# Adaptive-norm attention and gated FFN on one core: couple terms placed between the pairs of score tiles, with transfers in small parts

## The chip, the cores and the metric

The kernel runs on one core of one Trainium2 chip. The metric is device time in microseconds of one execution, the median of several runs. The kernel is written in Bass with Tile: the program names instructions and tiles, Tile adds the waits, and the order on TensorE (PE), VectorE (DVE), ScalarE (ACT) and of the transfers that SyncE (SP) issues is pinned to the program's order by small wrappers (`pe`, `dve`, `act`, `sp1`). [...]

## The reference, cut to what matters

The input is one sequence of 2048 rows of 512. Attention has 32 query heads of width 16 over a single key and value head; the FFN has a width of 1792.

```python
mod = (silu(c) @ w_mod).reshape(c.shape[0], 6, 1, -1)
sa, ca, ga, sb, cb, gb = mod[:, 0], ..., mod[:, 5]
h = layernorm(x) * (1 + ca) + sa
x = x + ga * A(h, A_wq, A_wk, A_wv, A_wo)        # q per head, one k, one v; softmax(q k / 4) v; @ wo
h = layernorm(x) * (1 + cb) + sb
x = x + gb * B(h, B_w_gate, B_w_up, B_w_down)    # (sigmoid(h Wg) * (h Wu)) Wd
```

Products of float32 operands are formed of float16 high and low parts in three passes (high x high, high x low, low x high), except the product of the probabilities with V, which is in float32.

## The kernel before, in words

**Stages.** A prologue (the word list `PLAN`) computes the modulation rows, the first norm, K, V and part of Q. A main loop then runs over 32 units: a unit is a block of 256 query rows (8 blocks) with one of 4 groups of 8 heads. A unit has 16 steps, one per 128 keys, and a step has two halves, here called pieces: 1024 pieces in all. An epilogue computes the last block's output projection and FFN with the whole 128x128 array.

**Attention in a piece.** The array is used as two halves of 64 rows, each with four column tiles of 32, so that a product 64x128x512 is a set of four matmuls side by side (`columns`, L137 to 139). `ORDER` (`"a0", "s0", "c", "a1", "s1"`) sets a piece: two score tiles `a` for the row maxima of a later unit (written to banks `sa`, three of them, reduced by DVE, `a_max`), two score tiles `s` with the keys on partitions (banks `st`, two of them, exponentiated by ACT into `P`, `st_tile`), and between the pairs `c`, the product of V with the probabilities of the step pair before (`pv`), into the one bank `craw`. The score tiles of a piece all stand on one array half; `pv` stands on the other, `side[0]`. Which is which changes at every second step (`sides`). [...]

**Couple terms.** Projections and the FFN of the blocks that are through with attention fill in. A `Couple` is two `Group`s (two row tiles) that run together, one on each array half; after half of its terms the two groups change halves (`g = self.gs[j ^ (n >= m)]`), behind a hand-over. A term is one set on either half. Per block there are: the output projection `wo` (24 terms, banks `po`), 7 gate-up couples `gu` (24 terms each, banks `pgu`) and two down couples `dn` (banks `pd`) of the hidden chunks below and from `HF` up: 48 and 36 terms with `HF = 8`. In `ffn_block`, the line `gs.insert(NCH, gs.pop(NCH - 1))` puts the first down couple ahead of the seventh gate-up couple. `pace` and `places` spread the terms over pieces at a rate of at least `LEAST` 2 and at most `MOST` 3, so that a block's work ends `CHAIN` 26 steps into the next block. `pick` takes a couple once all its inputs in `needs` are marked and `GAP` 2 steps have passed. `piece` plans and then issues one part of the running couple, after the piece's score tiles:

```python
for n in range(n0, n1):
    ...
    for j in (1 - side[0], side[0]):
```

**What comes between.** When a couple ends, its two banks are evicted by ACT and DVE (for `gu`: `th` twice and `u` once on ACT, `u` once on DVE). POOL then makes the float16 rows `gr`, which a transposing transfer on SP turns (`turned`, 3 steps later, `GLATE`). After `wo`, POOL and DVE do the second norm (`norm`, `norm2`, `norm3`, each deferred by steps) and make rows `h2r`, which are turned the same way (`HLATE`); a mark is set when the transfer is issued. Gate-up weights come from DRAM (`wD`) as 1 MB chunks into two buffers (`ask`, one transfer per chunk, issued as the couple before opens).

**Weights.** `weight_jobs` splits the FFN weights into high and low parts on POOL (L333 to L335) and stores gate and up to `wD`; 42 of the 46 jobs are spread over the first `WSTEPS` = 90 steps of the main loop.

Of the kernel before, what the change touches and what calls it, by code (L numbers as in the profile page):

```python
# [61 lines left out]

SKIP = 9
GAP = 2
CHAIN = 26
QRATE = 1.1
MOST = 3
# [1 line left out]
HELD = 60  # L69
SWAP = 5  # L70
FRESH = 0.9
WSTEPS = 90
WLAST = 100
WLATE = 2
WSTORE = 5
# [17 lines left out]
def adaln_mqa_glu_kernel(  # L93
# [100 lines left out]
    class Couple:  # L194
        def __init__(self, a, c):
            self.gs, self.stage, self.w, self.n = (a, c), a.stage, a.w, 2 * a.n

        def part(self, n0, n1):
            if n0 == 0:
                for g in self.gs:  # L200
                    g.open()
            m = self.gs[0].n
            for n in range(n0, n1):
                if n == m:
                    assert self.since is not None or done[0] > self.marks
                    take_over(self.since)
                for j in (1 - side[0], side[0]):
                    g = self.gs[j ^ (n >= m)]
                    l_, r_, *cut = g.term(n % m, slice(64 * j, 64 * j + 64))
                    columns(cut[0](g.bank) if cut else g.bank, l_, r_, n == 0, n == 2 * m - 1)  # L210
                if n == m - 1:
                    self.since, self.marks = None, done[0]
                    if open_[0]:
                        hand_over()
                        self.since = done[0]
            if n1 == self.n:
                for k, g in enumerate(self.gs):
                    g.end(g.bank, k == 1)
# [576 lines left out]

    use, gws = [0], {}

    def ask(upto):
        while use[0] <= upto:
            k = use[0]  # L800
            gws[k] = gw_tile()
            sp1.dma_start(gws[k], wD[CH[k % NCH]])
            use[0] += 1

    def ffn_block(b, end_of_all=False):
        x1, xrs, h2, ups, ths, gT = {}, {}, {}, {}, {}, {}
        at = b * NCH
        HF = 8

        def wo_group(t):  # L810
            def term(n, rs):
                o, i = divmod(n, 3)
                a_, w_ = passes(*aTs[b, o], WO['woh'], WO['wol'])[i]
                return a_[rs, t * P:(t + 1) * P], w_[rs, o, :]

            def begin():
                xrs[t] = t32("xr")
                sp1.dma_start(xrs[t], x[b * QU + t * P:b * QU + (t + 1) * P, :])

            def end(po, second):  # L820
                xr, t1 = xrs.pop(t), t32("t1")
                if second:
                    act.activation(t1, po, AF.Identity)
                    pool.tensor_tensor(t1, t1, mods[2], op=ALU.mult)
                else:
                    dve.tensor_tensor(t1, po, mods[2], op=ALU.mult)
                if tail:
                    dve.tensor_tensor(xr, t1, xr, op=ALU.add)
                    row_norm([t1], [xr])
                    dve.tensor_tensor(t1, t1, mods[4], op=ALU.mult)  # L830
                    dve.tensor_tensor(t1, t1, mods[3], op=ALU.add)
                    x1[t] = xr, t1
                else:
                    defer(1 + 2 * t, lambda: norm(t, t1, xr))

            return Group("wo", 12, "po", term, end, begin)

# [3 lines left out]

        def norm2(t, t1, xr):
            row_norm([t1], [xr], later=True)
            defer(1, lambda: norm3(t, t1, xr))

        def norm3(t, t1, xr):
            x1[t] = xr, t1
            pool.tensor_tensor(t1, t1, mods[4], op=ALU.mult)
            pool.tensor_tensor(t1, t1, mods[3], op=ALU.add)
            rows = pair("h2r")  # L850
            pool.tensor_scalar(rows[:, 0], t1, 1.0, 0.0, op0=ALU.mult, op1=ALU.add)
            pool.tensor_tensor(rows[:, 1], t1, rows[:, 0], op=ALU.subtract)
            h2[t] = turned(rows, f"h2{t}")
            if b == 0 and t == 0:
                ask(0)
            defer(HLATE, h2[t][1])

        def turned(rows, name):
            t_ = pair(name).rearrange("p a (c r) -> p (a c) r", r=P)

            def go():
                sp1.dma_start_transpose(t_, rows.rearrange("p a n -> p (a n)"))
                marks[b, name] = now[0]

            return t_, go

        def gu_group(c_, t):
            def begin():
                if t == 0:
                    ask(at + c_ + 1)  # L870
                    ths[c_], ups[c_] = t32("th"), t32("u")

            def term(n, rs):
                k, i = divmod(n, 3)
                gw = gws[at + c_]
                h_, w_ = ((0, 0), (1, 0), (0, 1))[i]
                return h2[t][0][rs, 4 * h_ + k, :], gw[rs, k, 2 * w_:2 * w_ + 2, :].rearrange("p m n -> p (m n)")

            def end(p_, second):
                ts = slice(256 * t, 256 * (t + 1))  # L880
                th, u_ = ths[c_], ups[c_]
                if second:
                    dve.tensor_copy(u_[:, ts], p_[:, 256:])
                    act.activation(th[:, ts], p_[:, :256], AF.Tanh, scale=0.5 / (SH * SW))
                else:
                    act.activation(th[:, ts], p_[:, :256], AF.Tanh, scale=0.5 / (SH * SW))
                    act.activation(u_[:, ts], p_[:, 256:], AF.Identity)
                if t == 1:
                    gated_rows(c_)

            return Group("gu", 12, "pgu", term, end, begin)

        def gated_rows(c_):
            th, u_ = ths.pop(c_), ups.pop(c_)
            pool.tensor_scalar(th, th, 1.0, 1.0, op0=ALU.add, op1=ALU.mult)  # L895
            pool.tensor_tensor(th, th, u_, op=ALU.mult)  # L896
            rows = pair("gr")
            pool.tensor_scalar(rows[:, 0], th, 1.0, 0.0, op0=ALU.mult, op1=ALU.add)
            pool.tensor_tensor(rows[:, 1], th, rows[:, 0], op=ALU.subtract)  # L899
            gT[c_], go = turned(rows, f"g{c_}")  # L900
            if tail:
                go()
            else:
                defer(GLATE, go)

        def gu_cols(c_, m):
            def begin():
                if m == 0:
                    ask(at + c_ + 1 if c_ < NCH - 1 else at + c_)

            def term(n, rs):
                e, (k, i) = n // 12, divmod(n % 12, 3)
                gw = gws[at + c_]
                h_, w_ = ((0, 0), (1, 0), (0, 1))[i]
                return gw[rs, k, 2 * w_ + m, e * P:(e + 1) * P], h2[k][rs, h_, :QU], lambda z: z[:, e * QU:(e + 1) * QU]

            def end(p_, second):
                if m == 0:
                    ths[c_] = th = t32("th")
                    act.activation(th, p_, AF.Tanh, scale=0.5 / (SH * SW))  # L920
                    return
                th, g_ = ths.pop(c_), pair("gc")
                dve.scalar_tensor_tensor(th, th, 1.0, p_, op0=ALU.add, op1=ALU.mult)
                pool.tensor_scalar(g_[:, 0], th, 1.0, 0.0, op0=ALU.mult, op1=ALU.add)
                pool.tensor_tensor(g_[:, 1], th, g_[:, 0], op=ALU.subtract)
                gT[c_] = g_

            return Group("gu", 24, "pgu", term, end, begin)
# [52 lines left out]
        for ds in downs:  # L981
            gs.append(Couple(*ds))
            gs[-1].needs = [(b, f"g{c_}") for c_ in (range(HF // 2) if len(gs) == NCH + 1 else range(NCH))]
        gs.insert(NCH, gs.pop(NCH - 1))
        first = Couple(*wos)
        for g in [first, *gs]:
            g.b = b
# [85 lines left out]
    def pick(s):  # L1073
        if urgent and s >= urgent[0].ready:
            return urgent.pop(0)
        if work and all(k in marks and s >= marks[k] + GAP for k in getattr(work[0], "needs", ())):
            return work.pop(0)

    def pace(s, g):
# [35 lines left out]
            at += z  # L1115
        assert at == g.n, (at, g.n, g.stage)

    def piece(s, h):
        plan(s, 2 * s + h)
        if run:  # L1120
            g, n0, n1 = run.pop(0)
            if n1 > n0:
                g.part(n0, n1)


    vq = []
# [2 lines left out]
    for i, (b, o) in enumerate(units):  # L1129
# [5 lines left out]
        for kb in range(NKB):  # L1135
# [13 lines left out]
            for n in range(2):  # L1149
                t = kb - kb % 2 + n  # L1150
                for z in ORDER:
                    k = int(z[1:] or 0)
                    if z[0] == "a" and an + 4 * n + 2 * k + 1 - h < len(alist):
                        a_tile(*alist[an + 4 * n + 2 * k + 1 - h])
                    if z == "c" and vq:
                        pv(*vq[n], second)
                    if z[0] == "s":
                        st_tile(i, t, k, 1 - h, second)
                if n == 0:
                    lows[:] = [z() for z in ready_rows]  # L1160
                piece(s, n)
                if n == 1:
                    for z in lows:
                        z()
# [8 lines left out]
                wdone += 1  # L1173
    assert wdone == nw and len(qdone) == 4 * NB
    while run:
        piece(s, 1)
    for n in range(4):
        pv(*vq[n % 2], n > 1)
    while waits:
        now[0] += 1  # L1180
        for z in [z for z in waits if z[0] <= now[0]]:
            waits.remove(z)
            z[1]()
    psum["ctx"].close()
    psum["ctx"] = ctx.enter_context(ExitStack())
    psum["b"] = psum["ctx"].enter_context(tc.tile_pool(name="pz", bufs=1, space=PSUM, reuse_waits="tile"))
# [47 lines left out]
```

## Time and profile before

| | |
|---|---|
| median of 3 runs | 1681.4 us (1678.07 to 1688.73) |
| the profiled execution | 1682.25 us |
| its span, first to last instruction | 1680.5 us |
| mean granted TensorE clock | 0.988 |
| PE, PEld busy | 1608.2 us, 991.0 us |
| DVE, ACT, POOL busy | 1419.8 us, 1305.5 us, 666.2 us |

In rows of the order of time, the first number is the start in us from the span's start, the second the time in us, then engine, line, operation, output and inputs, shape and count; a bracket gives the idle time before and what ended it. In the table by stretches a row gives the stretch, its length, then for PE, PEld (weight loads), DVE, ACT and POOL the busy time and the number of instructions, then the granted clock, the share of the DMA engines and GB/s. In the table of waits a row gives the total, the number of times and the longest. Nearly all instructions of PE, DVE, ACT and SP show line 139, that of a helper, so the tile names tell them apart.

### The profile page before, as it was taken

To read this page: it belongs to the slowest core of one execution; us is meant where nothing else is said; L and a number is where in the kernel's file an instruction comes from. 1 tells how busy PE (TensorE), PEld (TensorE's weight loads), DVE (VectorE), ACT (ScalarE), POOL (GpSimd) and SP (SyncE) were. 2 spreads that over 40 slices of the span, in tenths; PEclk is the share of its full clock that TensorE was granted. 3 is DMA by queue.
4 is the path that set the end of the run, shared out by engine and by line. 5 is a ranking of instruction groups with operands and counts; after the bars stand their busy time and mean duration, and the time that the engine had idled before them with its cause. 6 is when DMAs were issued, how large, how long until landed. Compare 5 with 4: busy or idle time off the path is not lost.

```text
span 1680.5 us, 91637 instructions
## 1 busy us (share of the span) xinstructions
PE 1608.2 (96%) x41477; PEld 991.0 (59%) x41477; DVE 1419.8 (84%) x2400; ACT 1305.5 (78%) x2409; POOL 666.2 (40%) x827
## 2 busy tenths in 40 slices
PE   6999999979999999999999999999999999999998
PEld 3335554436666566666566666666666666665465
DVE  7789999879999899999899999999899989993041
ACT  5549998768888888888888888888888888888600
POOL 4433756664315322362316331453226232442222
PEclk9989999989999999999999999999999999999999
DMA  7121433334321432233321341223322341233322
GB/s 243 57 69 43 126 130 125 93 99 127 85 59 28 113 81 52 57 89 84 78 59 35 116 104 24 59 86 83 82 59 65 84 103 54 29 112 83 108 76 75
DMA packets 145090, 140.18 MB, mean 83 GB/s; under 512 B 91332, under 2 KB 125116, under 8 KB 136636
## 3 DMA queue, kind: packets, MB, share of 16 engines
q1 hardware_dynamic: 144700, 134.32, 29.2%
q8 instruction: 325, 5.32, 1.3%
q14 instruction: 65, 0.53, 0.1%
HBM read 97.18 MB, written 16.24 MB: 67 GB/s over the span
## 4 chain that ended last, share of the span: by engine, by line
PE 81%; POOL 5%; ACT 4%; DVE 4%; DMA 3%; issue 2%; SPq 2%; POOLq 0%; ACTq 0%
PE craw L139 22%; PE pgu L139 17%; PE sa L139 16%; PE st L139 9%; PE pd L139 7%; PE po L139 3%; PE pgu L190 2%; PE pd L190 2%; PE pq L139 2%; DVE mx L139 2%; ACT P L139 2%; SPq L139 1%; POOL t L363 1%; DMA h<-h2r 1%; DMA xall<-in_A_x_dram 1%
## 5 line engine op out<-in xcount | busy, mean ns | idle before, releaser
L139 DVE TENSOR_REDUCE mx<-sa 128x1 f32<-128x512 f32 x2048 | 1310.0, 684 | 111.8 <-PE sa L139 56.3
L139 ACT ACTIVATE P<-st 128x512 f32<-128x512 f32 x2048 | 1180.5, 598 | 230.8 <-PE st L139 174.4
L139 PE MATMUL craw<-P,V 64*32 64x512 f32 x8192 | 1090.6, 598 | 2.1 <-issue 1.2
L139 PE MATMUL st<-qp,kp 64*32 64x512 f16 x8192 | 837.1, 380 | 11.3 <-ACT P L139 7.2
L139 PE MATMUL sa<-kp,qp 64*32 64x512 f16 (+1 forms) x7940 | 830.9, 379 | 8.9 <-DVE mx L139 5.5
L139 PEld LDWEIGHTS <-kp 64*32 64x32 f16 x8192 | 325.9, 91 | 262.5 <-issue 101.3
L139 PE MATMUL pgu<-gw,h 64*32 64x512 f16 x9408 | 422.2, 378 | 21.9 <-DMA h<-h2r 11.4
L139 PEld LDWEIGHTS <-qp 64*32 64x32 f16 (+1 forms) x7940 | 273.3, 92 | 139.7 <-issue 57.0
L139 PEld LDWEIGHTS <-h 64*32 64x32 f16 (+1 forms) x9600 | 211.8, 92 | 107.0 <-issue 41.7
L139 PEld LDWEIGHTS craw<-P,V 64*32 64x32 f32 x8192 | 194.8, 105 | 24.2 <-issue 5.1
L895 POOL TENSOR_SCALAR th<-th 128x512 f32<-128x512 f32 x49 | 30.3, 618 | 368.7 <-ACT th L139 242.6
L139 PE MATMUL pd<-wdh,g 64*32 64x512 f16 x2688 | 132.8, 377 | 0.8
L563 POOL MEMSET qp<- 32x1024 f16 x60 | 56.7, 944 | 131.7 <-PE st L139 129.7
L139 PEld LDWEIGHTS <-g 64*32 64x32 f16 x4032 | 86.7, 92 | 33.9 <-issue 6.7
L139 PE MATMUL pd<-wdl,g 64*32 64x512 f16 x1344 | 80.1, 376 | 0.0
L896 POOL TENSOR_TENSOR th<-th,u 128x512 f32<-128x512 f32 x49 | 62.9, 1284 | 4.1
L333 POOL TENSOR_SCALAR wst<-wst 128x512 f32<-128x512 f32 x46 | 28.4, 618 | 86.3 <-DMA wst<-in_B_w_gate_dram 28.8
L139 DVE COPY u<-pgu 128x256 f32<-128x256 f32 x49 | 20.3, 415 | 49.8 <-PE pgu L139 22.5
L948 POOL TENSOR_TENSOR ot<-ot,gb 128x512 f32<-128x512 f32 x12 | 15.4, 1282 | 115.9 <-ACT ot L139 115.9
L899 POOL TENSOR_TENSOR gr<-th,gr 128x512 f16<-128x512 f32 x49 | 57.1, 1164 | 4.0
L139 PE MATMUL craw<-nought 64*32 64x1 f16 x353 | 57.8, 164 | 0.0
L139 PE MATMUL pq<-h,wdh 64*32 64x512 f16 (+1 forms) x688 | 53.8, 386 | 0.1
(156 smaller groups left out, 1139.0 us busy)
## 6 DMA issues: line engine op xcount, KB each, us to landing
gw<-wD SPq DMA_DIRECT2D x56, 1024.0 KB
wD<-gw SPq DMA_DIRECT2D x7, 1024.0 KB
wm<-in_w_mod_dram SPq DMA_DIRECT2D x6, 1024.0 KB
qp<-qD SPq DMA_DIRECT2D x192, 32.0 KB
qD<-q SPq DMA_DIRECT2D x16, 256.0 KB
xr<-in_A_x_dram SPq DMA_DIRECT2D x16, 256.0 KB
out_dram<-ot SPq DMA_DIRECT2D x16, 256.0 KB
raw<-cs SPq DMA_DIRECT2D x248, 16.0 KB
```

The lines of the kernel that those rows point to most:

```text
L139: return (lambda *a, **k: keep(f_(*a, **k))) if pinned else f_
L190: pe.matmul(cut[0](self.bank) if cut else self.bank, l_, r_, start=(n == 0), stop=(n == self.n - 1))
L333: pool.tensor_scalar(w_, w_, SW, 0.0, op0=ALU.mult, op1=ALU.add)
L363: eng.tensor_scalar(dst, src, mv[:, i, 0:1], rs[:, i:i + 1], op0=ALU.subtract, op1=ALU.mult)
L563: eng.memset(qp[j:j + 32], 0.0)
L895: pool.tensor_scalar(th, th, 1.0, 1.0, op0=ALU.add, op1=ALU.mult)
L896: pool.tensor_tensor(th, th, u_, op=ALU.mult)
L899: pool.tensor_tensor(rows[:, 1], th, rows[:, 0], op=ALU.subtract)
L948: pool.tensor_tensor(ot, ot, mods[5], op=ALU.mult)
```

## The change

1. `Couple.part` is split. A new `front` is called right after `pv`, between the two pairs of score tiles. If the part holds two terms or more and is not the first of its couple, `front` issues the sets of the first half of its terms (rounded up) on the score tiles' half, `1 - side[0]`. `part`, after the second pair, issues the other sets: those left on the score half, and all on the other half. The wait of the change of halves, `take_over`, moves into `front` where there is one.
2. Transposes are issued in four parts of two 128-column blocks, and the gate-up chunk is loaded in eight parts of 128 KB. One of these parts is issued at the end of each piece (`drip`), transposes first; `fetched` issues what is left of a chunk when its couple opens.
3. `HF` is 6 instead of 8 (the down couples have 36 and 48 terms), and the seventh gate-up couple is no longer moved behind the first down couple.
4. The second norm of the second row tile starts one step earlier (`1 + t` instead of `1 + 2 * t`), and `norm3` becomes part of `norm2`, one step earlier for both.
5. `WSTEPS` is 66 instead of 90. For the first block, gate-up couples wait `EGAP` = 6 steps behind the mark of `h21` instead of `GAP` = 2.

```diff
+EGAP = 6
-WSTEPS = 90
+WSTEPS = 66
...
+        def half(self, n, j):
+            m = self.gs[0].n
+            g = self.gs[j ^ (n >= m)]
+            l_, r_, *cut = g.term(n % m, slice(64 * j, 64 * j + 64))
+            columns(cut[0](g.bank) if cut else g.bank, l_, r_, n == 0, n == 2 * m - 1)
+
+        def front(self, n0, n1):
+            self.ahead = 0
+            if n0 == 0 or n1 - n0 < 2:
+                return
+            m = self.gs[0].n
+            assert n1 <= m or n0 >= m
+            if n0 == m:
+                assert self.since is not None or done[0] > self.marks
+                take_over(self.since)
+            self.ahead = (n1 - n0 + 1) // 2
+            for n in range(n0, n0 + self.ahead):
+                self.half(n, 1 - side[0])
+
         def part(self, n0, n1):
...
-            m = self.gs[0].n
+            m, k = self.gs[0].n, self.ahead
+            if n0 == m and not k:
+                assert self.since is not None or done[0] > self.marks
+                take_over(self.since)
             for n in range(n0, n1):
-                if n == m:
-                    assert self.since is not None or done[0] > self.marks
-                    take_over(self.since)
-                for j in (1 - side[0], side[0]):
-                    g = self.gs[j ^ (n >= m)]
-                    l_, r_, *cut = g.term(n % m, slice(64 * j, 64 * j + 64))
-                    columns(cut[0](g.bank) if cut else g.bank, l_, r_, n == 0, n == 2 * m - 1)
+                if n + k < n1:
+                    self.half(n + k, 1 - side[0])
+                self.half(n, side[0])
...
+    turns, loads = [], []
+
+    def drip():
+        if turns:
+            turns.pop(0)()
+        elif loads:
+            loads.pop(0)[1]()
+
+    def fetched(upto):
+        while loads and loads[0][0] <= upto:
+            loads.pop(0)[1]()
...
-            gws[k] = gw_tile()
-            sp1.dma_start(gws[k], wD[CH[k % NCH]])
+            gws[k] = gw = gw_tile()
+            for z in range(NDC):
+                for y in range(2):
+                    at = slice(2 * y, 2 * y + 2)
+                    loads.append((k, lambda gw=gw, k=k, z=z, at=at: sp1.dma_start(gw[:, z, at], wD[CH[k % NCH], :, z, at])))
...
-        HF = 8
+        HF = 6
...
-                    defer(1 + 2 * t, lambda: norm(t, t1, xr))
+                    defer(1 + t, lambda: norm(t, t1, xr))
...
-            defer(1, lambda: norm3(t, t1, xr))
-
-        def norm3(t, t1, xr):
             x1[t] = xr, t1
...
+            def part(z):
+                sp1.dma_start_transpose(t_[:, 2 * z:2 * z + 2], of[:, 2 * z * P:2 * (z + 1) * P])
+                if z == 3:
+                    marks[b, name] = now[0]
+
             def go():
-                sp1.dma_start_transpose(t_, rows.rearrange("p a n -> p (a n)"))
-                marks[b, name] = now[0]
+                turns.extend(lambda z=z: part(z) for z in range(4))
...
                 if t == 0:
+                    fetched(at + c_)
                     ask(at + c_ + 1)
...
-        gs.insert(NCH, gs.pop(NCH - 1))
...
-        if work and all(k in marks and s >= marks[k] + GAP for k in getattr(work[0], "needs", ())):
+        if work and all(k in marks and s >= marks[k] + (EGAP if k == (0, "h21") else GAP) for k in getattr(work[0], "needs", ())):
...
-    def piece(s, h):
+    def front(s, h):
         plan(s, 2 * s + h)
+        if run and run[0][2] > run[0][1]:
+            run[0][0].front(*run[0][1:])
+
+    def piece():
         if run:
             g, n0, n1 = run.pop(0)
             if n1 > n0:
                 g.part(n0, n1)
+        drip()
...
-                    if z == "c" and vq:
-                        pv(*vq[n], second)
+                    if z == "c":
+                        if vq:
+                            pv(*vq[n], second)
+                        front(s, n)
```

In the epilogue a transpose is issued whole as its four parts at once, and `gu_cols` issues the next chunk's eight parts as a chunk opens.

More of the change, by code (lines that the diff above doesn't have):

```diff
@@ L859, in turned @@
             t_ = pair(name).rearrange("p a (c r) -> p (a c) r", r=P)
+            of = rows.rearrange("p a n -> p (a n)")
+            def part(z):
+                sp1.dma_start_transpose(t_[:, 2 * z:2 * z + 2], of[:, 2 * z * P:2 * (z + 1) * P])
+                if z == 3:
+                    marks[b, name] = now[0]
             def go():
-                sp1.dma_start_transpose(t_, rows.rearrange("p a n -> p (a n)"))
-                marks[b, name] = now[0]
+                turns.extend(lambda z=z: part(z) for z in range(4))
             return t_, go
@@ L900, in gated_rows @@
             gT[c_], go = turned(rows, f"g{c_}")
-            if tail:
-                go()
-            else:
+            if not tail:
                 defer(GLATE, go)
+                return
+            go()
+            while turns:
+                drip()
         def gu_cols(c_, m):
@@ L909, in begin @@
                     ask(at + c_ + 1 if c_ < NCH - 1 else at + c_)
+                    fetched(at + c_ + 1)
             def term(n, rs):
@@ L1123, in piece @@
                 g.part(n0, n1)
+        drip()
     vq = []
@@ L1160, in adaln_mqa_glu_kernel @@
                     lows[:] = [z() for z in ready_rows]
-                piece(s, n)
+                piece()
                 if n == 1:
@@ L1175, in adaln_mqa_glu_kernel @@
     while run:
-        piece(s, 1)
+        front(s, 1)
+        piece()
     for n in range(4):
@@ L1183, in adaln_mqa_glu_kernel @@
             z[1]()
+    while turns or loads:
+        drip()
     psum["ctx"].close()
```

## The prediction

> **What bounds the kernel now.** First the page, then a table by stretches, then the order of the instructions in single stretches, then the table of waits.
>
> ```profile
> span 1680.5 us, 91637 instructions
> ```
>
> What the array can do is seen in the order of time of PE in one quiet stretch (start, busy us):
>
> ```profile
> 667.37 0.40 PE L139 MATMUL sa<-kp,qp 64*32 64x512 f16 x4
> 667.41 0.64 PE L139 MATMUL craw<-P,V 64*32 64x512 f32 x4
> 667.58 0.40 PE L139 MATMUL st<-qp,kp 64*32 64x512 f16 x4
> 667.80 0.40 PE L139 MATMUL sa<-kp,qp 64*32 64x512 f16 x4
> 667.86 0.61 PE L139 MATMUL craw<-P,V 64*32 64x512 f32 x4
> 668.01 0.40 PE L139 MATMUL st<-qp,kp 64*32 64x512 f16 x4
> 668.23 0.46 PE L139 MATMUL pd<-wdl,g 64*32 64x512 f16 x8
> 668.44 0.68 PE L139 MATMUL pd<-wdh,g 64*32 64x512 f16 x16
> 668.88 0.40 PE L139 MATMUL sa<-kp,qp 64*32 64x512 f16 x4
> ```
>
> Four matmuls side by side make a set; sets on one array half follow each other by 0.216 us (667.37, 667.58, 667.80, 668.01, 668.23): call that a slot. The two sets of craw take two slots each, on the other half, at the same time. So a piece (half a step) costs 4 slots on either half, sa st sa st against craw craw, and each couple term, with a set on each half, one more. Here 7 slots, 1.51 us, with 3 terms: nothing is lost.
>
> ```profile
> 192.40:234.10 41.70, 40.73 (x1048) 22.16 (x1036) 39.84 (x70) 37.79 (x70) 23.80 (x30) 1.00 0.37 115
> 322.60:376.80 54.20, 44.41 (x976) 21.22 (x983) 41.81 (x74) 36.80 (x68) 37.08 (x49) 0.91 0.31 81
> 657.20:702.70 45.50, 45.27 (x1370) 30.69 (x1361) 42.92 (x71) 39.07 (x72) 11.17 (x13) 1.00 0.20 53
> 376.80:1583.90 1207.10, 1182.59 (x34366) 771.79 (x34349) 1068.30 (x1773) 1023.43 (x1903) 441.09 (x516) 1.00 0.30 75
> ```
>
> These are (us, then busy of PE, PEld, DVE, ACT, POOL) unit 2, unit 5, unit 12, and units 6 to 31 together. Unit 2 has one term a piece, which is 5 slots, 34.6 us for 32 pieces; it takes 41.7 because DVE is busy 39.84 of it: that is the floor that DVE sets, 1.30 us a piece. Units 6 to 31 are 832 pieces. Of their 34366 matmuls, 832 x 16 are st and craw, 790 x 8 are sa and some 350 are small; the other 14,400, eight to a term, are 1800 terms. (832 x 4 + 1800) x 0.216 is 1107.6 us, so **99.5 us** of the 1207.1 are lost against the slots. PE bounds that stage, DVE stands close behind it (42.92 busy of 45.50 in unit 12), and the losses are what a change of order can reach.
>
> **The change part by part.** The sum is made on the profiled execution, 1682.25 us (span 1680.5), which is 0.05% above the median 1681.4.
>
> *The first block's wait (EGAP 6, WSTEPS 66).*
>
> ```profile
> 355.71 1.24 SPq L139 DMA_TRANSPOSE h<-h2r  x1
> ...
> 358.77 1.04 PE L139 MATMUL pgu<-gw,h 64*32 64x512 f16 x12 [9.38 <-DMA h<-h2r]
> ```
>
> In unit 5 the first gate-up couple is started two steps after its transposes were meant to start, but POOL, behind with the weight splits, lets the second transpose go only at 355.71; PE stands 9.38 us and everything behind it in its queue, the score tiles too. With the splits done by step 66 and the couple four steps later the rows are there: **-9.4**. The price: eight pieces hold no terms, and their 16 go to units that PE bounds, 16 x 0.216 = **+3.5**; the eight pieces themselves stay at DVE's 1.30. Denser splits in units 0 to 4 press on POOL, whose work is not on the path there (23.8 of 41.7 busy): 0, with -3 to +5 kept.
>
> *Order and sizes of the down couples (HF 6, no reorder), the earlier second norm.* Before, the first down couple comes ahead of the seventh gate-up couple, and in every block the work runs dry before h2 is turned:
>
> ```profile
> 544.43 0.41 PE L139 MATMUL st<-qp,kp 64*32 64x512 f16 x4
> ...
> 549.37 0.40 PE L139 MATMUL st<-qp,kp 64*32 64x512 f16 x4
> ```
>
> Four pieces without a term, 4.94 us for 16 slots (3.46): 1.48 lost. Such a gap stands in units 9, 13, 17, 21, 25 and 29. After the change the piece of work left for behind wo is the second down couple of 48 terms instead of 36; at 1800/832 = 2.16 terms a piece that is 22 pieces in place of 17, five more than the gap, so it fills it: 6 x 1.48 = **-8.9**. The second norm goes one step up but its transposes, in quarters, one a piece, queue behind the first four, so the mark falls nine steps after wo's end as before: 0.
>
> *Small parts of transfers.* The waits of PE in units 6 to 31 (us, times, longest):
>
> ```profile
> PE pgu L139 <- issue: 7.0, 8, 1.9
> PE st L139 <- issue: 4.0, 4, 2.1
> PE sa L139 <- issue: 2.9, 3, 1.5
> ...
> PE pgu L139 <- DMA h<-h2r: 2.0, 2, 1.3
> ```
>
> 13.9 us are "issue": PE waits for nothing shown. The longest falls amid a set of four:
>
> ```profile
> 820.83 0.40 PE L139 MATMUL st<-qp,kp 64*32 64x512 f16 x3
> 821.18 0.16 PE L139 MATMUL craw<-nought 64*32 64x1 f16 x1
> 823.44 0.37 PE L139 MATMUL st<-qp,kp 64*32 64x512 f16 x1 [2.09 <-issue]
> ```
>
> and SP's queue had just issued:
>
> ```profile
> 816.49 0.38 SPq L139 DMA_DIRECT2D gw<-wD  x1
> ...
> 820.13 1.23 SPq L139 DMA_TRANSPOSE g<-gr  x1
> ```
>
> [...] Spread over eight and four pieces such bursts are thinner; bounds are none and all of 13.9, and since other issue waits stand behind small loads that stay, I take half, **-7**, and the two waits for h, **-2.0**. [...]
>
> More issues on SP: 392 further loads at 0.38 us and 189 further transposes at up to 1.23 are some 380 us on a queue that does nothing else; each is one a piece (1.3 us). The small transfers queued behind them (denominators, q tiles, maxima) have steps to spare. A gate-up couple lasts 24/2.16 = 11 pieces and asks for 8 loads and 4 quarters, so the last load is pushed out as the next couple opens; its first reader is that couple's tenth term, four pieces later. I take **+2**, from 0 to +12.
>
> *Half of the terms between the pairs.* Order of a piece with two terms, before: sa st craw craw sa st, then the terms. After: one term's set on the score half between the pairs. Score half: 4 + N sets either way; other half: craw, then N sets. No slot more or less, if a set on the other half may start past sets that wait for the score half. It may:
>
> ```profile
> 803.28 0.59 PE L139 MATMUL craw<-P,V 64*32 64x512 f32 x1
> 803.29 0.38 PE L139 MATMUL pgu<-gw,h 64*32 64x512 f16 x1
> 803.30 0.59 PE L139 MATMUL craw<-P,V 64*32 64x512 f32 x3
> 803.47 0.41 PE L139 MATMUL sa<-kp,qp 64*32 64x512 f16 x4
> 803.69 0.39 PE L139 MATMUL st<-qp,kp 64*32 64x512 f16 x2
> ```
>
> Here craw, issued after sa and st, starts 0.19 us ahead of the one and 0.41 ahead of the other: it passes two sets, as many as a piece of three terms will ask for.
>
> What it brings is even spacing. Now the two st sets start 0.43 us apart and then 0.87 or more, while one exp takes 0.6 on two banks; a hiccup of ACT shows at once, above all where a couple ends:
>
> ```profile
> 598.53 0.38 PE L139 MATMUL st<-qp,kp 64*32 64x512 f16 x4
> ...
> 600.60 0.40 PE L139 MATMUL st<-qp,kp 64*32 64x512 f16 x4
> ```
>
> ACT in that time:
>
> ```profile
> 598.82 0.38 ACT L139 ACTIVATE th<-pgu 128x256 f32<-128x256 f32 x1
> 599.09 0.39 ACT L139 ACTIVATE u<-pgu 128x256 f32<-128x256 f32 x1
> 599.51 0.38 ACT L139 ACTIVATE th<-pgu 128x256 f32<-128x256 f32 x1
> ```
>
> 2.07 us for a piece of 6 slots (1.30): 0.77 lost at some 65 couple ends, about 50 us, half of the 99.5. The first piece of a couple has no front, so the burst of three evictions (1.15 us) stays; with the st sets a slot later in steady pieces, some 0.2 us of slack before the next one replaces today's none. I take 0.15 us at each of 65 ends, **-10**; bounds 0 and 0.77 x 65 = -50, near the low end because ACT's own burst remains. Against it, take_over now stands before the front terms, so PE's queue waits for the hand-over matmul one couple in two legs, behind two sets rather than four: two sets cover 0.43 us, the hand-over waits for the last set of the other half (up to one slot) and takes 0.16; at most 0.1 us on each of 70 couples: **+3**, 0 to +7.
>
> *The tail.*
>
> ```profile
> 1630.05 15.94 PE L190 MATMUL pgu<-h2c,gw 128*128 128x256 f16 x144 [1.76 <-DMA gw<-wD]
> ```
>
> The loads in eighths let PE start when the first parts are there: **-1.5**. The couples left over are 36 and 48 terms instead of 48 and 36, the same 84; the shorter one first starts wo's rest 2.6 us earlier, and the longer one fills the norm behind: **-2**.
>
> Sum: -9.4 + 3.5 - 8.9 - 7 - 2 + 2 - 10 + 3 - 1.5 - 2 = -32.3, so **1650 us**.
>
> **The rivals.**
>
> *The even order does more.* If the spacing takes half of the 50 us at couple ends, it is 15 us more, and all issue waits 7 more: 1628. For it: unit 12, with few stalls, still takes 45.5 where its slots, 32 x 4 and (1370 - 32 x 24)/8 = 75 terms, are 43.8. Against: DVE at 42.92 leaves little below 44.
>
> *DVE takes over.* PE is freed, but the reduces' 1.30 us a piece plus the FFN's evictions is all there is to be had; the freed time comes back as waits for sa banks, and only the first block's stall (-5.9), the gaps (-8.9) and the tail (-3.5) stay, less +5 for SP and take_over: 1669. For it: 42.92 of 45.5 busy. Against: 26 units at 43 are still 89 us under the 1207.1.
>
> *The array halves are not free of each other: slower.* If matmuls start in program order, the other half's terms wait for the last front term and then run alone. At 2.16 terms a piece, some 136 pieces hold a third term and lose one slot (29 us); and where the halves change roles, every fourth piece, the score tiles wait for the set that lags, 208 x 0.216 = 45 us. Without the front's own terms (-10 + 3) the sum is 1657; with 74 more, 1731. It decides from the first piece with two terms. If only one set may be passed, just the 29 us come, 1686. Against both stand the rows at 803.28. [...]
>
> *It doesn't do what it says.* A piece with fewer than two terms, or the first of a couple, has no front; at 2.16 terms the others have one. Only if the plan put its terms into single pieces would nothing move; the quoted stretch speaks against it, so this gets no chance of its own.
>
> **How the numbers follow.** Forecast 0.56 (1650, own range 1632 to 1668); more from the even order 0.16 (1628); DVE takes over 0.19 (1669); halves not free 0.09 (1731, or 1686). A measurement of this kernel tells about 1% from no change, 16.8 us: faster means under 1664.6, slower over 1698.2. The forecast's range lies nine tenths below 1664.6 (0.50) and the even order wholly (0.16), DVE a fifth (0.04): faster 0.70. Same takes the rest of these and the weak form of the slower rival: 0.22; slower 0.08. The range for 8 in 10 goes from 1624, where the even order ends, to 1686, the weak form.
>
> **What would show it.** Right: PE's wait for h of 9.38 in unit 5 gone; stretches without terms in units 9, 13, ... gone; the issue sum of 13.9 halved; in a piece of two terms, sa st, one set, sa st, with the two st starts 0.65 apart; units of about 45.3 us in place of 46.4. Wrong: the other half idle after craw while front sets are pending (halves not free); DVE over 96% with sa waiting for it (DVE takes over); new waits of PE for gw at couple starts (loads too thin); or unit 4 and 5 longer, with POOL or wo late.

## The result, and the profile after

| | median us | lowest to highest | ratio to before |
|---|---|---|---|
| before | 1681.1 (4 runs) | 1678.07 to 1688.73 | |
| the change | 1748.6 (4 runs) | 1740.33 to 1757.64 | 1.0396 [1.0334, 1.0458] |

The change is **slower by 4%**, where 1650 us had been forecast. The profiled execution took 1740.33 us, at a mean granted clock of 0.972 (before 0.988).

From the page of the changed kernel, its span and the busy time of each engine:

```profile
span 1738.5 us, 92267 instructions
PE 1629.8 (94%) x41482; PEld 1029.0 (59%) x41482; DVE 1416.6 (81%) x2400; ACT 1312.4 (75%) x2409; POOL 666.1 (38%) x827
```

PE is busy 21.6 us longer, and the span is 58.0 us longer: more time is spent waiting, and the same work runs slower. The table by stretches says where. Before, units 4 and 5, and unit 13:

```profile
276.80:376.80 100.00, 86.95 (x1948) 42.59 (x1955) 82.69 (x142) 73.78 (x136) 63.82 (x82) 0.93 0.34 100
702.70:747.20 44.50, 44.17 (x1299) 29.29 (x1289) 43.28 (x75) 38.72 (x70) 27.34 (x34) 1.00 0.26 65
```

After, unit 2, unit 12, units 10 and 11, units 4 and 5, and units 6 to 31:

```profile
192.90:234.50 41.60, 40.66 (x1043) 22.28 (x1032) 39.95 (x69) 37.79 (x70) 33.16 (x42) 1.00 0.53 170
660.60:705.60 45.00, 44.78 (x1355) 30.87 (x1341) 42.79 (x72) 40.00 (x73) 11.67 (x13) 1.00 0.18 48
554.90:660.60 105.70, 96.07 (x2684) 65.33 (x2672) 85.84 (x143) 80.14 (x153) 29.46 (x35) 0.95 0.31 81
276.80:359.90 83.10, 81.55 (x1843) 40.62 (x1846) 81.70 (x142) 73.66 (x136) 35.76 (x47) 1.00 0.21 56
359.90:1645.00 1285.10, 1208.79 (x34477) 811.43 (x34462) 1065.08 (x1773) 1030.82 (x1904) 443.30 (x518) 0.97 0.28 72
```

Units 4 and 5 are 16.9 us shorter (100.0 to 83.1), what follows unit 31 is 3.1 shorter (1738.5 - 1645.0 against 1680.5 - 1583.9), and units 6 to 31 are 78.0 longer (1285.1 against 1207.1). Unit 12, in which few rows are fetched and turned, is even 0.5 shorter; units 10 and 11 take 105.7 us, in which PE is busy only 96.07. So the loss sits in the FFN's middle part, in some units and not in others. The table of waits for units 6 to 31 after the change (us in total, times, longest):

```profile
PE pgu L140 <- DMA gw<-wD: 59.6, 20, 6.8
PE pgu L140 <- DMA h<-h2r: 4.1, 5, 1.2
PE pgu L140 <- ACT u L140: 2.7, 12, 0.5
PE st L140 <- DMA qp<-mh: 2.7, 1, 2.7
```

Before, no wait for gw stood in this stage. Now PE waits 20 times for a gate-up chunk, 59.6 us, and the 13.9 us of "issue" that stood there are gone from the table. The order of time of SP's queue in unit 10 tells why (start, us, instruction, count; `raw`, `lD` and `lc` move the last unit's attention results and their denominators, `qp` the q tiles, `gw` the gate-up chunk, `g` the turned rows):

```profile
561.03 1.15 SPq L140 DMA_DIRECT2D lD<-cs  x2
562.23 5.70 SPq L140 DMA_DIRECT2D raw<-cs  x8
567.97 1.97 SPq L140 DMA_DIRECT2D gw<-wD  x2
570.05 2.49 SPq L140 DMA_TRANSPOSE g<-gr  x2
572.58 1.04 SPq L140 DMA_DIRECT2D lc<-lD  x1
573.73 2.46 SPq L140 DMA_TRANSPOSE g<-gr  x2
576.23 3.88 SPq L140 DMA_DIRECT2D qp<-qD  x6
580.15 2.61 SPq L140 DMA_DIRECT2D gw<-wD  x5
582.87 0.37 SPq L140 DMA_DIRECT2D lD<-rc  x1
583.28 0.91 SPq L140 DMA_DIRECT2D gw<-wD  x2
```

Each row begins where the one above ends: SP issues for 23 us with no pause of half a microsecond. The quarter transposes hold it 1.24 us each. A gate-up couple starts on PE at 572.97. The last three eighths of its chunk go out only from 580.15 on, 7.2 us later, behind two quarter transposes and six q tiles (the other two loads of that row are the next chunk's). PE, in the same stretch:

```profile
577.00 0.42 PE L140 MATMUL pgu<-gw,h 64*32 64x512 f16 x4
577.07 0.61 PE L140 MATMUL craw<-P,V 64*32 64x512 f32 x4
582.60 0.62 PE L140 MATMUL pgu<-gw,h 64*32 64x512 f16 x4 [4.91 <-DMA gw<-wD]
582.98 0.67 PE L140 MATMUL sa<-kp,qp 64*32 64x512 f16 x4
583.40 0.67 PE L140 MATMUL st<-qp,kp 64*32 64x512 f16 x4
```

It stands 4.91 us, until the first of these three eighths has landed, 2.4 us after it was issued; and the score tiles, which need no chunk, stand behind it in its queue.

The other 19 waits look the same. The part waited for is always one of the last four of its chunk. From 10 us before each wait until that part was issued, SP was issuing 83 to 95% of the time. The part landed 2.4 to 3.9 us after its issue (worked out from the semaphore counts in the trace), sooner than any whole chunk of this stage before the change, 4.8 to 7.9 us. So the small loads are not slow as transfers; they go out late.

After the wait the sets follow each other by 0.42 us instead of 0.21: the wait is paid for a second time, as the granted clock, the third number from the end, shows over four stretches (577.20 to 582.60 holds the wait):

```profile
570.00:577.20 7.20, 7.08 (x213) 4.61 (x196) 6.69 (x13) 6.41 (x13) 3.67 (x4) 1.00 0.34 80
577.20:582.60 5.40, 0.49 (x14) 0.00 (x0) 0.53 (x1) 0.60 (x1) 0.02 (x1) 0.86 0.30 83
582.60:587.60 5.00, 5.00 (x80) 2.61 (x83) 1.90 (x3) 1.59 (x3) 0.00 (x0) 0.50 0.61 174
587.60:592.60 5.00, 5.00 (x153) 3.31 (x149) 4.40 (x8) 3.99 (x8) 1.81 (x3) 0.96 0.22 45
```

PE is busy throughout the third stretch, at a clock of 0.50, and starts 80 instructions in it, where the fourth, at 0.96, has 153. The same trace has the 0.50 after a wait of only 2.67 us, too (PE goes on at 1368.60, and from 1369.6 the clock is 0.50); others of 2.27 and 2.67 us (ended at 428.97 and 412.18) did not cost the clock.

### The profile page after: what moved, and what is told of

It reads as the page before. It is cut to its first block, busy times and chain, and to the rows that moved or that the text cites. A ratio compares the mean times of both kernels' runs of the same rounds, so it can differ in the third digit from the quotient of the medians.

```text
span 1738.5 us, 92267 instructions
## 1 busy us (share of the span) xinstructions
PE 1629.8 (94%) x41482; PEld 1029.0 (59%) x41482; DVE 1416.6 (81%) x2400; ACT 1312.4 (75%) x2409; POOL 666.1 (38%) x827
## 4 chain that ended last, share of the span: by engine, by line
PE 68%; SPq 9%; issue 5%; DVE 5%; DMA 5%; POOL 5%; ACT 3%; POOLq 0%; ACTq 0%; DVEq 0%
PE craw L140 18%; PE sa L140 12%; PE pgu L140 12%; PE st L140 10%; SPq L140 8%; PE pd L140 5%; DVE mx L140 3%; DMA gw<-wD 3%; PE po L140 2%; PE pq L140 2%; PE pd L191 2%; PE pgu L191 2%; ACT P L140 1%; DMA h<-h2r 1%; POOL t L382 1%
## 5 line engine op out<-in xcount | busy, mean ns | idle before, releaser
L140 PE MATMUL st<-qp,kp 64*32 64x512 f16 x8192 | 853.6, 383 | 9.0 <-ACT P L140 5.7
L140 PE MATMUL sa<-kp,qp 64*32 64x512 f16 (+1 forms) x7940 | 848.5, 383 | 6.0 <-DVE mx L140 5.6
L140 PE MATMUL pgu<-gw,h 64*32 64x512 f16 x9408 | 605.1, 386 | 70.5 <-DMA gw<-wD 59.6
L140 PEld LDWEIGHTS <-kp 64*32 64x32 f16 x8192 | 307.8, 92 | 224.6 <-issue 88.3
L140 PEld LDWEIGHTS <-h 64*32 64x32 f16 (+1 forms) x9600 | 253.1, 93 | 168.3 <-issue 111.7
L140 PE MATMUL pd<-wdh,g 64*32 64x512 f16 x2688 | 190.5, 376 | 1.2 <-DVE t L140 0.2
L140 PEld LDWEIGHTS <-g 64*32 64x32 f16 x4032 | 105.8, 92 | 26.9 <-issue 6.2
L140 PE MATMUL pd<-wdl,g 64*32 64x512 f16 x1344 | 112.9, 376 | 0.0
L738 POOL TENSOR_TENSOR raw<-raw 128x256 f32<-128x256 f32 x31 | 22.8, 735 | 180.6 <-DMA raw<-lD 72.5
L140 PE MATMUL po<-woh,a 64*32 64x512 f16 x896 | 63.8, 377 | 0.3
```

What stands on the lines that cost most here:

```text
L140: return (lambda *a, **k: keep(f_(*a, **k))) if pinned else f_
L738: keep(pool.tensor_tensor(raw[:, :QU], raw[:, :QU], raw[:, QU:], op=ALU.mult))
```

## The experiments

The theory after the result: the time is lost on **SP's queue**, to the number of its instructions, and not on the array. The rivals: the small loads are slow or late by their place or size as transfers, or the half-way terms cost the array its slots. All ratios are to the kernel before, which took 1684.0 us beside the first four experiments that follow, and 1681.9 or 1681.0 beside the others. Where two experiments are compared with each other, their ratios are the safer measure.

**Both transfers whole, the rest as in the change.**

```diff
-                turns.extend(lambda z=z: part(z) for z in range(4))
+                sp1.dma_start_transpose(t_, of)
+                marks[b, name] = now[0]
...
-            for z in range(NDC):
...
+            sp1.dma_start(gw, wD[CH[k % NCH]])
```

> The change, but with transposes and gate-up chunks issued whole and where they were before; all else (front, HF, EGAP, WSTEPS, norms) stays. Theory Q (SP's queue is held by the many issues: 1.43 us for a quarter of a transpose, as for a whole one, 0.50 for each eighth of a chunk): the waits of PE for gw (59.6 us) go, units with gate-up come back from 53 us to 46, time 1640 to 1660. Theory F (the half-way terms cost, because the array halves are not free of each other): those units stay over 50 us, time above 1700.

Measured: 1660.7 us (1660.31 to 1663.26), 0.9877 [0.9853, 0.9902]. The small parts alone cost 88 us (1748.6 against 1660.7), more than the whole loss; all else in the change gains 1.2%. The waits for gw are gone. The four largest waits of PE in its units 6 to 31:

```profile
PE pgu L140 <- issue: 5.5, 6, 1.3
PE st L140 <- issue: 2.7, 2, 2.0
PE st L140 <- ACT P L140: 2.2, 2, 1.3
PE sa L140 <- issue: 2.1, 2, 1.1
```

Its stretch of units 6 to 31 has the full clock, and its unit 13 has more terms in it than before (x1351 matmuls for x1299) in nearly the same time, as no piece is left without work:

```profile
361.60:1564.50 1202.90, 1180.81 (x34430) 800.15 (x34408) 1063.79 (x1773) 1030.49 (x1903) 444.67 (x518) 1.00 0.29 76
687.40:732.20 44.80, 44.75 (x1351) 30.99 (x1345) 43.33 (x74) 38.42 (x69) 26.77 (x34) 1.00 0.22 62
```

**One kind of part at a time.** First the transposes whole, in the first of their four slots, the eighth loads left where they are:

```diff
-                turns.extend(lambda z=z: part(z) for z in range(4))
...
+                turns.extend([whole, lambda: None, lambda: None, mark])
```

> The change with each transpose issued whole in the first of its four slots, the other three slots left empty, so that the loads in eighths keep their places in the program. Theory Q: SP loses 189 issues of 1.43 us, 270 us, its share in gate-up units falls from 80% to about 58%, and most of the 59.6 us of waits for gw go: 1655 to 1685. Theory S (the loads stand too late in the program, whatever SP does): unchanged within 1%, 1730 to 1760. Theory P (loads in rows of 1 KB land too slowly): unchanged too.

Measured: 1676.7 us, 0.9971 [0.995, 0.9991]. The loads keep size, number and place, and the waits for gw fall from 59.6 us to 22.9:

```profile
PE pgu L140 <- DMA gw<-wD: 22.9, 13, 4.6
PE pgu L140 <- ACT u L140: 2.7, 12, 0.5
```

So neither the size of the loads nor their place in the program makes most of the wait; the quarter transposes ahead of them in the queue do. Then the loads whole and the transposes in quarters:

```diff
-            for z in range(NDC):
...
+            sp1.dma_start(gw, wD[CH[k % NCH]])
```

> The change with chunks loaded whole where they were before, and transposes still in quarters. Theory Q: SP loses 392 issues of 0.50 us, but keeps the quarters; the whole load is issued as the couple before opens and has 15 us: the waits for gw nearly go, 1650 to 1680; small transfers behind the quarters still come late. Theory S and theory P: the same gain from the loads' place and size, 1640 to 1660, with nothing left that the quarters cost.

Measured: 1676.3 us, 0.9958 [0.994, 0.9976]. No wait for gw, but waits of "issue" as before the change (6.8, 2.9 and smaller, 13.8 in all). Each half of the edit alone costs 16 us against the kernel with both whole, and both together 88: they do not add. That is what a queue would do that has room for the one or the other. All of SP's transfer issues sum to 636 us before and with both whole, 851 with the loads alone in parts, 921 with the transposes alone, and 1106 with both. What the 16 us of the quarter transposes alone are made of is not shown; PE's waits for h there sum to 3.2.

What each instruction costs SP shows in the view of one tile's instructions on it (duration in ns: least, median, most). Before:

```profile
L139 SPq DMA_TRANSPOSE g<-gr x49: 1232/1270/2675, 382.7 to 1586.3; - x49
L139 SPq DMA_DIRECT2D gw<-wD x50: 321/374/1527, 335.3 to 1567.1; - x50
```

After:

```profile
L140 SPq DMA_TRANSPOSE g<-gr x196: 1167/1243/2404, 379.4 to 1645.4; - x196
L140 SPq DMA_DIRECT2D gw<-wD x400: 319/431/1907, 330.9 to 1635.5; - x134
```

A quarter of a transpose holds the queue about as long as the whole (1243 ns for 1270), and a load of 128 KB (431 ns) about as long as one of 1 MB (374 here; 354 and 520 in the two kernels above that load whole chunks). Added up, transposes take 358.7 us of SP for 91.0 (those of h counted) and gw's loads 224.6 for 25.0: 467 us more. In units 10 and 11 SP issues for 80.8 of 105.7 us, before for 39.5 of 94.9.

**The half-way terms.** The change without them, small parts kept:

```diff
-            if n0 == 0 or n1 - n0 < 2:
-                return
+            return
```

> The change without the half-way terms: the front issues nothing, all terms follow the second pair as before; small parts stay. Theory Q: the waits for gw stay, within 1.5% of the change, 1725 to 1775. Theory F: most of the loss goes, below 1700.

Measured: 1743.4 us (1741.03 to 1745.98), 1.0364 [1.034, 1.0389]. The largest row of PE's waits is still that for gw:

```profile
PE pgu L140 <- DMA gw<-wD: 66.7, 22, 6.3
```

The loss stays without them, so they are not its cause. The same edit with both transfers whole:

> The version with transposes and loads whole, and no half-way terms: all terms after the second pair. If the half-way terms bring what the prediction took for them (-10 + 3): 1664 to 1672. If they bring nothing, as in the pair with small parts (1743.4 without, 1748.6 with): 1656 to 1663. If they cost: below 1656.

Measured: **1649.9 us** (1645.8 to 1657.1), 0.9815 [0.9782, 0.9848]: the lowest median of all, 1.8% under before, and 10.9 under the same kernel with half-way terms. The reverse, the kernel before with half-way terms alone:

> The kernel before with the half-way terms alone. Theory L (the set of the other half that now runs last lags, and the score tiles wait for it where the halves change roles: 0.08 us more in 200 such pieces, as the medians 0.195 and 0.117 of the versions with both whole show, 16 us, less some 5 saved elsewhere): 1686 to 1696. The prediction's step (-10 + 3): 1672 to 1676. Nothing either way: 1678 to 1685.

Measured: 1689.4 us, 1.0054 [1.0034, 1.0075]: they cost 8.5 us there, clear of the noise, where the prediction had 7 us of gain. The sign is the same in each of the four pairs that differ in them: +10.9, +8.5, +5.2 (1748.6 against 1743.4, small parts) and +3.1 (below). The last two are not to be told from nothing, as the intervals of their ratios overlap.

Where they cost it was worked out from the starts of the sets of sa, st and craw in 789 pieces of units 6 to 30, each piece's time less its slots. In three of four pieces nothing is lost with them (median -0.001 us). In each fourth, at whose end the score tiles change to the other half, the median is 0.196 with them and 0.115 without (both transfers whole; means 0.230 and 0.184, so 9 us in 197 pieces), and in the kernel before 0.132 and 0.108. In these pieces craw starts 0.120 us behind sa with them and 0.090 without: the other half runs further behind the score half. The theory was that the score tiles wait for it as the halves change roles. If so, leaving the half-way terms out of the last piece ahead of a change should help:

```diff
-            run[0][0].front(*run[0][1:])
+            g, n0, n1 = run[0]
+            g.front(n0, n0 if h == 1 and s % 2 == 0 else n1)
```

> Transposes whole, chunks in four parts, half-way terms in all pieces but those after which the halves change roles. Theory L: the loss of those pieces is back at the median of 0.12, the even spacing stays in the rest, and the time is that without half-way terms or a little under it: 1640 to 1648. If the half-way terms cost something else: 1650 to 1657, as with all of them.

Measured: 1655.9 us, 0.9853 [0.9829, 0.9877], against 1655.1 with them there (the kernel with chunks in four parts, below): no gain. The loss in the pieces ahead of a change stayed at 0.196, with the lag at 0.161: the pieces before may have built it up already. The place of the loss holds; that the last piece makes it does not, and that the lag is its cause is not shown.

**Loads in four parts, transposes whole.**

```diff
-                for y in range(2):
...
+                loads.append((k, lambda gw=gw, k=k, z=z: sp1.dma_start(gw[:, z], wD[CH[k % NCH], :, z])))
...
-                turns.extend(lambda z=z: part(z) for z in range(4))
+                sp1.dma_start_transpose(t_, of)
+                marks[b, name] = now[0]
```

> The change with each transpose whole (one slot) and each chunk loaded in four parts instead of eight. Theory Q, with its second half (the issue waits of PE, 13.9 us before, 10.9 in the version with both whole, come from loads of 1 MB, and were about 1 us with eighths): SP's issue time in gate-up units about 25 us of 46, no waits for gw, issue waits under 5: 1645 to 1660, at or below the version with both whole (1660.7). If parts of loads do harm by themselves: 1665 to 1680.

Measured: 1655.1 us, 0.9845 [0.9826, 0.9863], 5.7 less than with loads of 1 MB, though the intervals of the two ratios overlap. The issue waits are 5.1 us for 10.9, the largest row of them:

```profile
PE pgu L140 <- issue: 3.0, 5, 1.0
```

Without half-way terms:

> Transposes whole, chunks in four parts, no half-way terms; the rest as in the change. If the two gains add (10.9 us without the half-way terms, 5.7 with chunks in four): 1642 to 1648. If they are the same time gained twice: 1648 to 1653.

Measured: 1652.0 us (1648.93 to 1654.85), 0.9826 [0.9802, 0.985], against 1649.9 with whole loads: the gain of 5.7 does not come on top. Issue waits were 8.5 here for 11.1. Whether four parts help at all stays open.

**The first block.** Both transfers whole, and the old sizes:

```diff
-EGAP = 6
+EGAP = 2
-WSTEPS = 66
+WSTEPS = 90
```

> The version with transposes and loads whole, with WSTEPS back at 90 and EGAP at 2. The prediction's step: the first block's wait comes back, +9.4 - 3.5 = 6, or up to 12 as the rows of units 4 and 5 (17 us shorter with the change) less the terms that moved would have it: 1666 to 1673. If the gain was given back later: 1658 to 1663.

Measured: 1669.0 us, 0.9936 [0.9914, 0.9959], so the new sizes are worth 8.3 us in this kernel. PE waits there once, longer than the 9.38 before the change:

```profile
PE pgu L140 <- DMA h<-h2r: 14.9, 1, 14.9
```

**The order of the couples.** Both transfers whole, `HF` back at 8 and the seventh gate-up couple behind the first down couple:

```diff
-        HF = 6
+        HF = 8
...
+        gs.insert(NCH, gs.pop(NCH - 1))
```

> The version with transposes and loads whole, with HF back at 8 and the first down couple ahead of the seventh gate-up couple again. The prediction's step: gaps of four pieces without terms return in six units, 8.9 us: 1667 to 1672. If the gap is closed by other means (the norm one step earlier) or DVE takes it: 1658 to 1664.

Measured: 1708.3 us, 1.0166 [1.0149, 1.0183]: 47.6 more, far from what either theory gave. So it doesn't measure the gaps without terms. In the table of waits for units 6 to 31:

```profile
PE pgu L140 <- DMA h<-h2r: 24.9, 6, 4.5
```

With the old order the work runs dry sooner while the second norm starts by its new step; the next gate-up couple is opened as soon as its mark allows, its rows are not yet turned, and PE waits once in each of six blocks. After these waits, too, the clock falls: it stands at 0.50 for 30.7 us of the stage, and PE is busy in 26.7 of them. That suggests that the earlier norm needs the new order to cover its chain; the two were not taken apart further. The gaps themselves are counted instead: pieces without a term in units 6 to 30 are 24 before, 3 after the change and none with whole transfers.

## Why the prediction was wrong, point by point

**The step that failed** is the one on SP: "some 380 us on a queue that does nothing else; each is one a piece (1.3 us). The small transfers queued behind them ... have steps to spare", and from it **+2**, from 0 to +12. It measured +88, net of the issue waits that the small parts took away. Its size of the added work was near (467 for 380). What was missing is the time that was there to take it: the queue's load per unit was not set beside the unit's length. SP was not idle; its q tiles, denominators and maxima come in bursts (the 5.70 us of eight `raw` loads at 562.23), and in units 10 and 11 its 39.5 us became 80.8. The prediction's own count, 12 parts in a couple of 11 pieces at one a piece, already said that some loads go out only as their couple opens; "the last load is pushed out as the next couple opens" and "four pieces later" for its reader were too kind: in unit 10 three parts of eight were left, PE wanted the first of them 4.7 us after the couple's start (at 577.69), and SP, with transposes and q tiles ahead of it, sent it after 7.2. Nor was a wait of PE priced with the clock: of the 78 us in units 6 to 31 some 49 are waits (59.6 for gw, 2.1 more for h, 2.7 for qp, less 15.1 of issue waits), and the rest, about 29 us, is what all else nets to, the granted clock of 0.97 above all; that split is an estimate. The trace bears it out: in these units the clock stands at 0.50 twelve times, 68 us together, and PE is busy in 52 of them, half of which, as the sets' spacing of 0.42 us for 0.21 has it, is an estimated 26 us lost. Before, the clock stood at 1.00 in this stage.

**The issue waits** (-7): right in direction, too small in size. In units 6 to 31 they are 15.1 us before (13.9 in the rows shown), 9.1 to 13.8 in the other six kernels with loads of 1 MB, 5.1 to 8.5 in the three with 256 KB, and 0 to 0.5 in the three with 128 KB. So they go with the size of the loads; cutting the transposes alone left 13.8. In the three with 128 KB PE also waits for gw, so size is not all that differs there. What PE waits for in them no run shows, and so no run shows what the -7 rests on; its size was the author's estimate, half of 13.9. What the parts of 128 KB gave, the 15.1 less at most 0.5, was far less than their issues cost.

**The waits for h** (-2.0): wrong in the change, 4.1 for 2.0, since the quarter transposes stand in the same queue; right where both are whole, no such row being left.

**The half-way terms** (-10 + 3): wrong in sign, +3 to +11. What they do was seen rightly: the halves pass each other, and the order is that foretold. From the order of time of PE after the change:

```profile
673.73 0.41 PE L140 MATMUL sa<-kp,qp 64*32 64x512 f16 x4
673.83 0.64 PE L140 MATMUL craw<-P,V 64*32 64x512 f32 x4
673.94 0.41 PE L140 MATMUL st<-qp,kp 64*32 64x512 f16 x4
674.16 0.41 PE L140 MATMUL pd<-wdh,g 64*32 64x512 f16 x4
674.28 0.61 PE L140 MATMUL craw<-P,V 64*32 64x512 f32 x4
674.37 0.41 PE L140 MATMUL sa<-kp,qp 64*32 64x512 f16 x4
674.59 0.41 PE L140 MATMUL st<-qp,kp 64*32 64x512 f16 x4
```

The two st sets stand 0.65 us apart (673.94, 674.59), craw at 673.83 starts ahead of the st set issued before it, and no slot of the score half is empty. The same rows show the lag: craw starts 0.10 us behind sa (673.73). But the even order bought nearly nothing: losses of over 0.3 us a piece sum to 46 to 51 us with and without them (both transfers whole), so ACT's burst at couple ends was not softened by the 0.2 us of slack. What they cost appears where the halves change roles, and goes with the lag of the other half there; the one test of that lag missed, so the cause stays open. In the prediction such a cost stood only as part of the rival in which halves aren't free; it comes though they are free.

**The first block** (-9.4 + 3.5 = -5.9): right in kind, PE's wait of 9.38 gone. Taking the step back cost 8.3, but there the wait was 14.9, so 8.3 is no measure of the 9.38. The two units became 16.9 us shorter and not 9.4, since the clock was slower, too (0.93 over the 100 us before, 1.00 after): PE was busy for 8.7 us at 0.50 (5.25 of them from 353.8 to 364.0, around that wait, and 3.41 behind a wait of 2.49 that ended at 308.47), which is some 4.3 lost, and some 2.8 are terms that moved out (1948 to 1843 matmuls); both are estimates.

**The order and the gaps** (-8.9): borne out as far as it can be separated. The gaps went from 24 pieces to 3 or none. In the kernel with both transfers whole and no half-way terms, units 6 to 31 are 13.8 us shorter than before (1193.3 against 1207.1); taking off the issue waits (4.0), the waits for h (2.0) and adding the 3.5 of terms moved in leaves some 11 us for this step, an estimate by what is left over, with the earlier norm and all else unpriced in it.

**The tail** (-1.5 - 2): right in sum, -3.1 for -3.5. With whole loads and the new order it is already -2.6 (1658.5 - 1564.5, 94.0 for 96.6), so the eighths give about 0.5 here and not 1.5. The wait at its first couple is shorter, 1.09 for 1.76:

```profile
1690.18 14.68 PE L191 MATMUL pgu<-h2c,gw 128*128 128x256 f16 x132 [1.09 <-DMA gw<-wD]
```

**The rivals.** DVE did not take over (81% busy). "Halves not free" gave 1731, close to what came, by a mechanism that isn't there: three of four pieces lose nothing (median -0.001 us). That a price comes out right is no proof. What the prediction named as the sign of its failure, "new waits of PE for gw at couple starts (loads too thin)", is what the table of waits showed first, and it had been given no rival and no chance of its own.

Without the two wrong terms the sum comes near: with +2 - 10 + 3 taken out, and -4 in place of -7 for the issue waits, as measured with loads of 1 MB, it gives 1658, and the kernel with both transfers whole and no half-way terms took 1649.9. That this is the 1650 that had been forecast for the whole change is luck: the terms that were wrong stand in for 8 us that this sum does not explain.

## What to carry to other kernels

Before splitting a transfer, take the issue time of each instruction on its queue from the trace, and set the sum against the length of the busiest stretch, not of the whole run: here 80.8 us of issues in 105.7 were already too many, because they come in bursts and the loads with a date stand behind those without. Price a new wait of TensorE with the clock that the trace grants after it as well: here 0.50 for the 5 us behind a wait of 4.91 us. Where two streams share the array halves and change roles, look at how far the one lags at the change before adding work ahead of the other: here 0.120 us with the added work and 0.090 without, beside a loss of 0.196 and 0.115.

## What the runs showed of the hardware

- A transpose by DMA holds SP's queue 1.24 us for a quarter and 1.27 us for the whole, a plain load 0.43 us for 128 KB and 0.35 to 0.52 us for 1 MB (medians).
- A load of 128 KB landed 2.3 to 5.2 us after the start of its issue, one of 1 MB 4.8 to 7.9 us (units 6 to 31, from the semaphore counts).
- After a wait of 4.91 us the clock of TensorE was granted at 0.50 for the 5 us that followed, and at 0.96 in the 5 us after that; a wait of 2.67 us had the same effect once, and once had not.
- PE's issue waits shrink as single loads get smaller: 9.1 to 15.1 us of units 6 to 31 with 1 MB, 5.1 to 8.5 with 256 KB, 0 to 0.5 with 128 KB; cutting the transposes alone left 13.8. What they are is not shown.
- Two halves of the array that lose nothing side by side (median -0.001 us a piece) still lose 0.11 to 0.20 us (medians) at each change of roles, where one runs 0.09 to 0.16 us behind the other.
